# RWKV-6 attention and a gated feed-forward layer: idle products out of the first stage, two blocks of small products moved on TensorE

## The chip, the cores and the metric

The kernel runs on one core of one Trainium2 chip. The metric is the time of one execution on the device in microseconds (us), lower is better; a kernel's time is the median of its runs. The core has five engines with an instruction list each: PE (TensorE, matrix products; PEld is its loading of the stationary operand), DVE (VectorE), ACT (ScalarE), POOL (GpSimd) and SP (SyncE, which here only issues DMAs).

## The reference

Two blocks in a row, all in float32. First a recurrence over 768 tokens for 4 batches and 8 heads of width 48, then a feed-forward layer with an unusual activation over the 3072 tokens of width 384:

```python
for t in range(S):
    cur = np.einsum('bhd,bhe->bhde', u[None] * kt, vt)
    y[:, :, t] = np.einsum('bhd,bhde->bhe', rt, state + cur)
    state = wt[:, :, :, None] * state + np.einsum('bhd,bhe->bhde', kt, vt)
...
h = x @ w_in                                              # x: y as (3072, 384); w_in: (384, 2048)
sp = np.maximum(h, 0.0) + np.log1p(np.exp(-np.abs(h)))    # softplus
g = h * erf(sp)
return (g @ w_out).astype(np.float32)                     # w_out: (2048, 384)
```

## The kernel before

**Steps.** The 768 tokens are cut into 12 steps of 64 tokens; a step holds all 32 heads. `attend_first` (line 853) does step 0, `attend` (line 984) steps 1 to 4, `attend_late` (line 803) steps 5 to 11.

**Inside a step.** The decayed products of r and k of two tokens of a step are not made token by token but in six levels: level n takes the pairs of tokens that lie in the two halves of one block of 2^n tokens. Per level, `level_products` (line 646) issues 32 small matmuls into one of two PSUM banks (`products`, line 132, hands them out in turn), `take_level` (line 664) or a masked multiply puts what belongs to the level into the tile `own`, and `scale` (line 319) multiplies r and k by the decay of the level, in place, so that the next level can use them. Level 1 uses copies of r and k into which u is multiplied (`prepare`), so it needs nothing of `scale`. The decays themselves are made on POOL (line 357).

**From a step's products to x.** `from_own` (line 681) multiplies `own` by v into the PSUM tile `y`, in two halves called swap 1 and swap 0, 16 matmuls each. `fence` (line 697) is a small DVE copy that reads `y` between the halves. `through_state` (line 704) adds r times the state of the steps before (32 matmuls, line 713; nothing in step 0), copies `y` out on ACT (lines 721, and 741 or 751) and makes x transposed, `xT`. In steps 1 and later the rows that lie on other partitions are moved by six DMAs (line 757). In step 0 that is done by `hop` (line 726): three matmuls with a constant (`shift`, line 732) and three DVE additions (line 746). `state_part` (line 762) makes k times v of the step (32 matmuls, line 769), and `next_state` (line 620) adds it to the faded state on DVE, which step s+1 reads.

**Feed-forward.** `hidden` (line 1097) multiplies `w_in` by `xT` (line 1130, moving operand 256 columns wide) and ACT copies the result (line 1139); softplus and erf run on ACT; `project` (line 1161) and, from step 3 on, `project_fast` (line 1243) multiply by `w_out`. Pieces of these stand between the levels of a later step, so that PE has wide products to do while DVE scales.

**Weights.** `w_in` and `w_out` arrive as 64-bit words and are turned into float32 by ACT, DVE and POOL (`convert`, line 221, lines 259, 261, 267, 276, 281, 289) during steps 0 to 3. Each load of a pair of weight tiles is held back by a one-element copy (lines 240, 242) until some other result is there; `stages["l"](2, seen[:, 0:1])` in line 925, for example, stands behind the fence of step 0.

**What sets the order.** Everything lies in a manual schedule: on every engine the instructions stand in the order of the Python calls, and semaphores hold an instruction back until its inputs are there. Nothing overtakes on an engine. A float32 matmul of the program is recorded as two passes, each with a load of weights and a matmul, so PE executes four instructions for one call. The instructions themselves are brought to the core by DMA, on queues of their own.

**Products without a use.** Before the first real product PE runs 36 matmuls of 64x64 on the identity (line 1522, `FEW`) and five of 128x256 (`stay_warm`, line 967); two more `stay_warm` follow each half of level 1. Behind levels 2 to 5 of step 0 stands one product of 384 columns with a zero operand (`keep_busy`, line 976), which writes into the bank that the next level overwrites.

**The places that the change touches.** At the end of `attend_first`, after the products of level 6 (line 911), three eighths of the level 1 products of step 1 stand ahead of `from_own(0, own, 1)` (line 916) and five eighths between `through_state` and `hop` (line 940). At the end of `attend`, for steps 1 to 4, the order on PE is swap 1, the transposes of k (line 1051), a piece of `hidden`, `state_part`, swap 0, a piece, `through_state`.

Of the kernel before, what the change touches and what calls it, by code (L numbers as in the profile page):

```python
# [11 lines left out]
FP32 = mybir.dt.float32  # L12
# [5 lines left out]
P = 128  # L18
FAST = 3
EP = 64  # L20
HC = 64
NC = 2
NJ = 2
FG = 8
FT = 2
FEW = 36

# [33 lines left out]
def kernel(  # L63
# [14 lines left out]
    nc = tc.nc  # L78
    PSUM = bass.MemoryType.PSUM

    n_steps, _, _, JP, C = rkw.shape
# [4 lines left out]
    _, NT, DM = w_out.shape  # L86
# [27 lines left out]
    ident = const.tile([P, P], FP32, name="ident")  # L114
# [17 lines left out]
    def products(shape, n=None):  # L132

        if n is None:
            n = turns["next"]
            turns["next"] = 1 - n
        names = "abc"[: len(shape) - 1]
        return banks[n][:].rearrange(
            f"p ({' '.join(names)}) -> p {' '.join(names)}", **dict(zip(names, shape[1:]))
        )  # L140
# [167 lines left out]
    def rows(e, n=D):  # L308
        return slice(e * EP, e * EP + n)
# [336 lines left out]
    def level_products(pp, rk, level, ns=range(NJ * NP)):  # L646

        half = 1 << (level - 1)
        m = HC - half if 1 < level <= MASKED else HC if level == 1 else half
        for n in ns:  # L650
            for s0 in range(0, C, HC):
                for e in range(NE):
                    right = rk(0, n)[rows(e), s0 : s0 + HC]
                    to = pp[s0 : s0 + m, e, n, :]
                    if level > 1:
                        right = rights(right, half)
                        to = to[:, : HC // 2].rearrange("p (b h) -> p b h", h=half)
                    nc.tensor.matmul(  # L658
                        to, lhsT=rk(1, n)[rows(e), s0 : s0 + m], rhs=right,
                        start=True,  # L660
                        stop=True,
                    )
# [18 lines left out]
    def from_own(s, own, swap):  # L681
        vt = loaded[s][1]
        for j in range(NJ):
            for q in range(0, NP, 2):
                for h in range(NC):
                    e = h ^ swap
                    for p in (q, q + 1):
                        n = j * NP + p
                        t = slice(h * HC, (h + 1) * HC)
                        nc.tensor.matmul(  # L690
                            y[at(e, p), e, p // 2, j, t],
                            lhsT=vt[t, n * NE + e, :], rhs=own[t, e * JP + n, :],
                            start=swap == 1 and not j and not q, stop=True,
                            skip_group_check=True,
                        )
# [157 lines left out]
    def attend_first(xT):  # L853


        for _ in prepare(0):
            pass
        totals = plan_totals(0)
        _, vt, made, _, _ = parts_of(0)
        t5 = turns["first"]  # L860
        own = att.tile([P, NH, HC], FP32, name="own")
        halves = [range(j * NP, (j + 1) * NP) for j in range(NJ)]
        batch = JP * C // 2 // NJ
        pp = products([P, NE, JP, HC])
        for half in halves:
            level_products(pp, by_pair(made), 1, half)
            stay_warm(2)
        nc.scalar.copy(first[:], mask_sb[:, 0, :])
        totals(1, part=slice(0, batch))
        for j in range(NJ):  # L870
            scale(0, 1, batch=j)
        load_second(t5[:, 1, 0, NP - 1, 1:2])

        def wait_for(t):

            nc.gpsimd.tensor_copy(out=block_sb[:, 0:1], in_=t5[:, 1, 0, NP - 1, t : t + 1])

        wait_for(1)
        totals(1, part=slice(batch, 2 * batch))
        totals(2, part=slice(0, batch // 2))  # L880
        nc.vector.tensor_mul(
            own[:], pp[:].rearrange("p e n t -> p (e n) t"),
            first[:, None, :].to_broadcast([P, NH, HC]),
        )
        behind = {3: (3,), 4: (4, 5), 5: (6,)}
        for level in range(2, LOG):
            pp = turns.pop("pp", None) or products([P, NE, JP, HC])
            for j, half in enumerate(halves):
                level_products(pp, first_pair, level, half)
                scale(0, level, batch=j)  # L890
            turns["pp"] = products([P, NE, JP, HC])
            keep_busy(turns["pp"])
            take_level(own, pp, level)
            wait_for(1 << level - 1)
            if level == 2:
                totals(2, part=slice(batch // 2, batch))
            else:
                totals(*behind[level])
            if level == 2:
                stages["b"](0, 0)  # L900
                stages["b"](0, 1)
                stages["r"](0)
                for _ in prepare(1):
                    pass
                nc.sync.dma_start(out=vt[:], in_=v[0])
                stages["l"](1, own[:, 0, 2:3])
                nc.sync.dma_start(out=ws[1][:], in_=rkw[1][:, 2])
        totals = plan_totals(1)
        pp = turns.pop("pp")
        for half in halves:  # L910
            level_products(pp, first_pair, LOG, half)
        half = 1 << LOG - 1
        got, of = pp, own[:].rearrange("p (e n) t -> p e n t", e=NE)
        turns["pp"] = products([P, NE, JP, HC])
        second = by_pair(ready[1][0])
        level_products(turns["pp"], second, 1, range(3))
        for swap in (1, 0):
            for h in range(NC):
                some, e = slice(h * HC, h * HC + half), h ^ swap
                nc.scalar.copy(of[some, e, :, half:], got[some, e, :, :half])  # L920
        stages["h"](0)
        stages["h"](0)
        from_own(0, own, 1)
        fence()
        stages["l"](2, seen[:, 0:1])
        load_v(1)
        stages["o"](0)
        stages["b"](1, 0)
        stages["b"](1, 1)
        from_own(0, own, 0)  # L930
        view_k = view(t5[:, 0, 1], 0, [[2 * NP * C, NJ], [HC, NP * NC], [1, HC // 2]])
        tot = ready[0][1][LOG - 1]
        nc.vector.tensor_mul(
            view_k, view_k, view(tot, 1, [[NP * C >> LOG - 1, NJ], [2, NP * NC], [0, HC // 2]])
        )
        stages["h"](1)
        stages["h"](1)
        totals(1)
        through_state(0, xT)
        level_products(turns["pp"], second, 1, range(3, JP))  # L940
        turns.pop("hop")()
        stages["r"](1)
        stages["o"](1)
        totals(*range(2, LOG + 1))
        kT = att.tile([P, NH, D], FP32, name="kT", bufs=1)

        def turn():

            ps = products([P, JP, P], turns["next"])
            for n in range(JP):  # L950
                nc.tensor.transpose(ps[:, n, :], first_pair(1, n), ident[:])
            nc.scalar.copy(
                kT[:].rearrange("p (e n) d -> p e n d", e=NE),
                ps[:].rearrange("p n (e d) -> p e n d", e=NE)[..., :D],
            )
            send("br")
            load_third()
            stages["l"](5, kT[:, 0, 0:1])

        def to_state():  # L960
            ps = products([P, NC, JP, HC], turns["next"])
            state_part(0, kT, ps)
            next_state(0, ps)

        turns["pending"] = {2: turn, 3: to_state}
# [7 lines left out]
                start=True, stop=True,  # L973
            )

    def keep_busy(pp):

        zeros = states[0][:].rearrange("p h n d -> p (h n d)")
        nc.tensor.matmul(
            pp[:].rearrange("p e n t -> p (e n t)")[:, :DM], lhsT=ident[:],  # L980
            rhs=zeros[:, :DM], start=True, stop=True, skip_group_check=True,
        )

    def attend(s, xT, early, place, behind):
# [61 lines left out]
                nc.sync.dma_start(out=loaded[2][0][:, level - 3], in_=rkw[2][:, level - 3])  # L1046

        from_own(s, own, 1)
        ps = products([P, JP, P])
        for n in range(JP):  # L1050
            nc.tensor.transpose(ps[:, n, :], K[:, n, :], ident[:])  # L1051
# [10 lines left out]
            for _ in range(3):  # L1062
                mixing.send(nc.vector)

        ps = products([P, NC, JP, HC])
        state_part(s, kT, ps)
        from_own(s, own, 0)
        next_state(s, ps)
        for _ in following:
            pass  # L1070
        place(LOG + 1)
        through_state(s, xT)
        behind()

    later, chunks, started = [], [], []
# [435 lines left out]
    for kk in range(KT):  # L1511
        n = D // KT
# [3 lines left out]
    with tc.manual_schedule(  # L1516
        engines={getattr(mybir.EngineType, x) for x in ("PE", "DVE", "Activation", "Pool", "SP")}
    ):
        few = ps_m.tile([P, NC, P], FP32, name="m")
        for n in range(FEW):  # L1520
            here = rows(n & 1, HC)
            nc.tensor.matmul(
                few[here, 0, :HC], lhsT=ident[here, here], rhs=ident[here, here],
                start=True, stop=True,
            )
        stay_warm(5)
        for t in states:
            nc.gpsimd.memset(t[:], 0.0)
        nc.gpsimd.memset(over_blocks[:], 1.0)
# [176 lines left out]
```

## Time and profile before

| | |
|---|---|
| time, median of 3 runs | 585.51 us (583.67 to 587.04) |
| the profiled execution: its own time | 584.51 us |
| its span, first to last instruction | 582.7 us |
| mean granted TensorE clock | 0.994 |
| busy: PE, PEld, DVE, ACT, POOL | 98%, 85%, 73%, 61%, 42% |
| instructions recorded | 16637, of which 7304 matmul passes and as many loads of weights |

A row of the timeline is: start in us, length in us, engine, line, operation, output<-inputs, shape of weights, shape of moving operand, number of passes; in brackets the idle time of the engine before it and what the profile takes for its release. "issue" as a releaser means that the engine waited for nothing that the profile shows. Ends of matmuls are modelled, so a row may seem to reach into the next. In a table of stretches the columns are start and end, length, busy time of PE, PEld, DVE, ACT and POOL with the number of instructions, the granted clock of TensorE, the share of the 16 DMA engines that were busy, and GB/s.

How PE's time lies by stage, from such a table (busy of PE in each stretch):

| stretch, us | what | PE busy | clock |
|---|---|---|---|
| 2.00 to 8.40 | idle products | 6.40 of 6.40 | 1.00 |
| 8.40 to 21.40 | step 0, levels 1 to 6 | 11.49 of 13.00 | 1.00 |
| 21.40 to 30.40 | end of step 0, first products of step 1 | 6.58 of 9.00 | 0.62 |
| 30.40 to 65.50 | step 1, first half of step 2 | 34.33 of 35.10 | 1.00 |
| 65.50 to 100.00 | steps 2 and 3 | 34.25 of 34.50 | 1.00 |
| 100.00 to 582.70 | the rest | 479.22 of 482.70 | 1.00 |

### The profile page before, as it was taken

The page shows a single profiled execution, that of the slowest core. Times are in us where ns is not written, and L with a number is a line of the kernel's source. Part 1 is how long each engine was busy: PE and PEld are TensorE (multiplying, and loading weights), DVE is VectorE, ACT ScalarE, POOL GpSimd, SP SyncE. Part 2 cuts the span into 40 slices and gives each one's busy share as a digit, 9 for nine tenths or more (in the row PEclk, how much of TensorE's full clock was granted, in tenths as well). Part 3 has the DMA queues.
Part 4 walks back from the last instruction along what each step waited for, and adds up shares of the span by engine and source line. Part 5 has one row for each costly group of instructions (what it writes and reads, how often), then busy time and mean ns, then how long its engine had stood idle before and what let it go on. Part 6 is the DMA issues. An engine that isn't in the chain of part 4 may idle for free.

```text
span 582.7 us, 16637 instructions
## 1 busy us (share of the span) xinstructions
PE 572.3 (98%) x7304; PEld 493.7 (85%) x7304; DVE 426.8 (73%) x451; ACT 355.0 (61%) x478; POOL 242.1 (42%) x263
## 2 busy tenths in 40 slices
PE   8799999999999999999999999999999999999997
PEld 7588787678668758898898898898898899988997
DVE  7585794899795699699599599599599526356640
ACT  3567778635544597766766666665765761388700
POOL 3378273612793786276176077077074000000000
PEclk9799999999999999999999999999999999999999
DMA  7497472540435215236236336235331101000111
GB/s 258 137 340 268 158 235 67 207 154 12 145 79 163 86 48 181 46 119 191 47 112 197 47 110 199 46 110 163 47 108 29 19 10 36 0 2 1 28 28 27
DMA packets 52057, 62.04 MB, mean 106 GB/s; under 512 B 33392, under 2 KB 38800, under 8 KB 50960
## 3 DMA queue, kind: packets, MB, share of 16 engines
q1 hardware_dynamic: 51360, 60.58, 33.9%
q8 instruction: 57, 0.93, 0.6%
q10 hardware_dynamic: 624, 0.39, 0.3%
q14 instruction: 16, 0.13, 0.1%
HBM read 51.60 MB, written 8.27 MB: 103 GB/s over the span
## 4 chain that ended last, share of the span: by engine, by line
PE 86%; DMA 2%; DVE 0%; ACT 0%; issue 0%; SPq 0%; ACTq 0%
PE m L1130 31%; PE m L1243 28%; PE m L1161 11%; PE pp L1331 4%; PE pp L658 3%; PE y L1331 2%; PE y L690 2%; PE y L713 2%; PE pp L769 1%; DMA words<-in_moe_w_out 1%; PE pp L1051 1%; PE pp L1243 0%; DMA xT<-y 0%; PE pp L782 0%; DVE y L276 0%; DVE w_out_sb L281 0%
## 5 line engine op out<-in xcount | busy, mean ns | idle before, releaser
L1130 PE MATMUL m<-xT,w_in_sb 128*128 128x256 f32 x960 | 214.2, 381 | 1.0 <-ACT y L261 0.8
L1130 PEld LDWEIGHTS m<-xT,w_in_sb 128*128 128x128 f32 x960 | 180.0, 190 | 26.2 <-ACT y L261 0.8
L335 DVE TENSOR_TENSOR in<-in,tot_sb 128x1024 f32<-128x1024 f32 (+1 forms) x55 | 77.0, 1399 | 21.3 <-PE pp L658 20.7
L1139 ACT COPY h<-m 128x512 f32<-128x512 f32 x80 | 46.2, 580 | 63.0 <-PE m L1130 62.8
L1161 PE MATMUL m<-w_out_sb,h 128*128 128x384 f32 x192 | 64.3, 491 | 0.0
L1161 PEld LDWEIGHTS m<-w_out_sb,h 128*128 128x128 f32 x192 | 35.7, 190 | 23.5
L1243 PE MATMUL m<-mixed,h 128*128 128x192 f32 x256 | 45.6, 331 | 0.0
L1243 PE MATMUL m<-w_out_sb,h 128*128 128x192 f32 x256 | 44.8, 329 | 0.0
L1243 PEld LDWEIGHTS m<-mixed,h 128*128 128x128 f32 x256 | 41.4, 190 | 0.9
L1090 ACT ACT_TABLE_LOAD x30 | 38.5, 1283 | 5.9 <-DVE h L1095 5.4
L1243 PEld LDWEIGHTS m<-w_out_sb,h 128*128 128x128 f32 x256 | 41.6, 190 | 0.3
L658 PEld LDWEIGHTS pp<-in 48*48 48x48 f32 (+4 forms) x2368 | 30.3, 120 | 13.5 <-issue 6.8
L1243 PE MATMUL m<-w_out_sb,room 128*128 128x192 f32 x240 | 41.5, 326 | 0.0
L465 POOL TENSOR_TENSOR words<-words,own 128x384 f32<-128x384 f32 x21 | 31.0, 1476 | 22.5 <-DVE words L496 12.8
L1086 ACT ACT_TABLE_LOAD x30 | 38.5, 1283 | 2.3 <-issue 1.8
L458 POOL TENSOR_TENSOR own<-rest 128x384 f32<-128x384 f32 x7 | 10.4, 1481 | 71.0 <-ACT o L1249 59.7
L506 POOL TENSOR_TENSOR words<-words 128x384 f32<-128x384 f32 x28 | 39.7, 1446 | 0.0
L1243 PEld LDWEIGHTS m<-w_out_sb,room 128*128 128x128 f32 x240 | 39.4, 190 | 0.0
L658 PE MATMUL pp<-in 48*48 48x32 f32 (+4 forms) x2368 | 34.1, 206 | 2.1 <-issue 2.1
L618 POOL COPY faded<-s 128x1 f32<-128x1 f32 x10 | 12.4, 1240 | 54.5 <-DVE s L624 54.5
L531 DVE TENSOR_REDUCE sums<-rk 128x16 f32<-128x768 f32 (+2 forms) x31 | 31.7, 1022 | 0.0
L506 POOL TENSOR_TENSOR rk<-words 128x384 f32<-128x384 f32 x28 | 31.5, 1153 | 0.0
(202 smaller groups left out, 990.4 us busy)
## 6 DMA issues: line engine op xcount, KB each, us to landing
in<-in_rkw SPq DMA_DIRECT2D x8, 1024.0 KB, 5.0
words<-in_moe_w_in SPq DMA_DIRECT2D x16, 384.0 KB, 5.3
words<-in_moe_w_out SPq DMA_DIRECT2D x16, 384.0 KB, 6.2
words<-in_rk_rows SPq DMA_DIRECT2D x8, 768.0 KB, 7.2
w<-in_rkw SPq DMA_DIRECT2D x11, 512.0 KB, 6.5
v<-in_v SPq DMA_DIRECT2D x12, 384.0 KB, 5.4
out<-o SPq DMA_DIRECT2D x45, 96.0 KB, 2.5
in<-in_rkw SPq DMA_DIRECT2D x7, 512.0 KB, 5.8
```

The lines of the kernel that those rows point to most:

```text
L335: nc.vector.tensor_mul(halves, halves, view(tots[level - 1], 0, [[1, n], [2, nb], [0, half]]))
L465: engine.tensor_mul(to, to, of[:, :, None, :].to_broadcast([P, NEAR // 2 // half, half, D]))
L506: engine.tensor_mul(to[:, i], r[:, half:], k[:, part * rows + i, None].to_broadcast([P, half, D]),)
L531: nc.vector.tensor_reduce(out=to, in_=of, axis=mybir.AxisListType.X, op=ALU.add)
L658: nc.tensor.matmul(to, lhsT=rk(1, n)[rows(e), s0 : s0 + m], rhs=right, start=True, stop=True,)
L1086: nc.scalar.activation(sp_room, chunks[0], AF.Softplus)
L1090: nc.scalar.activation(at, sp_room, AF.Erf)
L1130: nc.tensor.matmul(ps[:, ff, :], lhsT=w_in_sb[:, g * FG + f + ff, kk * P : (kk + 1) * P], rhs=xT[:, kk, :], start=kk == 0, stop=kk == KT - 1,)
L1139: nc.scalar.copy(h[:, f : f + FT, :], ps[:])
L1161: nc.tensor.matmul(ps[j][:], lhsT=gs[g][:, f, j * C : (j + 1) * C], rhs=w_out_sb[:, g * FG + f, :], start=g + f == 0, stop=g == NG - 1 and ...
L1243: nc.tensor.matmul(to, lhsT=a[:, f], rhs=b[:, f], start=start and f == 0, stop=f == FG - 1, skip_group_check=True,)
L1331: nc.tensor.matmul(to[:, e], lhsT=a[:, 2 * i + e], rhs=b, start=start and not k, stop=True, skip_group_check=True,)
```

## The change

- The 36 matmuls of 64x64 at the start go; `stay_warm` runs six times in place of five.
- Behind level 6 of step 0, the three eighths of the level 1 products of step 1 are replaced by one `keep_busy` of 256 columns (it now takes its width). All 32 matmuls of that level stand in one piece behind the three `shift` products of `hop`, so swap 1, swap 0 and the shifts of step 0 follow each other on PE.
- In step 1 alone, `state_part` and `next_state` stand behind `through_state`: on PE swap 1, transposes, a piece of `hidden`, swap 0, a piece, `through_state`, `state_part`; on DVE `next_state` directly ahead of the first `scale` of step 2, as before with nothing between them. A `fence` is added between swap 1 and swap 0 of step 1.

No other engine's list changes its order: DVE gains the one fence; ACT, POOL and SP have the same instructions in the same order. PE loses 72 passes at the start and gains two there and two behind level 6.

```diff
-FEW = 36
@@ attend_first
         turns["pp"] = products([P, NE, JP, HC])
         second = by_pair(ready[1][0])
-        level_products(turns["pp"], second, 1, range(3))
+        keep_busy(turns["pp"], NC * P)
         for swap in (1, 0):
...
         through_state(0, xT)
-        level_products(turns["pp"], second, 1, range(3, JP))
         turns.pop("hop")()
+        level_products(turns["pp"], second, 1)
         stages["r"](1)
@@ keep_busy
-    def keep_busy(pp):
+    def keep_busy(pp, n=DM):
         zeros = states[0][:].rearrange("p h n d -> p (h n d)")
         nc.tensor.matmul(
-            pp[:].rearrange("p e n t -> p (e n t)")[:, :DM], lhsT=ident[:],
-            rhs=zeros[:, :DM], start=True, stop=True, skip_group_check=True,
+            pp[:].rearrange("p e n t -> p (e n t)")[:, :n], lhsT=ident[:],
+            rhs=zeros[:, :n], start=True, stop=True, skip_group_check=True,
         )
@@ attend
         from_own(s, own, 1)
+        if s == 1:
+            fence()
         ps = products([P, JP, P])
...
-        ps = products([P, NC, JP, HC])
-        state_part(s, kT, ps)
+        def to_next():
+            ps = products([P, NC, JP, HC])
+            state_part(s, kT, ps)
+            return ps
+
+        ps = to_next() if s > 1 else None
         from_own(s, own, 0)
-        next_state(s, ps)
+        if s > 1:
+            next_state(s, ps)
         for _ in following:
             pass
         place(LOG + 1)
         through_state(s, xT)
+        if s == 1:
+            next_state(s, to_next())
         behind()
@@ the start
-        few = ps_m.tile([P, NC, P], FP32, name="m")
-        for n in range(FEW):
-            here = rows(n & 1, HC)
-            nc.tensor.matmul(
-                few[here, 0, :HC], lhsT=ident[here, here], rhs=ident[here, here],
-                start=True, stop=True,
-            )
-        stay_warm(5)
+        stay_warm(6)
```

## The prediction

> **What bounds the kernel now.** I read the page first: engines, granted clock, DMA queues.
>
> ```profile
> span 582.7 us, 16637 instructions
> PE 572.3 (98%) x7304; PEld 493.7 (85%) x7304; DVE 426.8 (73%) x451; ACT 355.0 (61%) x478; POOL 242.1 (42%) x263
> PEclk9799999999999999999999999999999999999999
> q8 instruction: 57, 0.93, 0.6%
> ```
>
> PE is busy 98% of the span, and the chain that ended last is PE work from 76 us on; what it waits for before that is small (0.77 us at 65.49, 0.25 us at 75.94). So a microsecond gained before the first product of the feed-forward layer (30.40 us) reaches the end, unless it is given back on the way. The page also shows one slow slice of the clock, and a queue q8 that brings instructions: 57 packets for 14608 recorded instructions of PE, so 256 instructions or 128 passes to a packet. The second view is PE's timeline up to 30 us:
>
> ```profile
> 2.00 4.10 PE L1522 MATMUL m<-ident 64*64 64x64 f32 x72 [2.00 <-POOL ident masks.py:199]
> 6.03 2.43 PE L971 MATMUL m<-ident 128*128 128x256 f32 x10
> 8.38 0.69 PE L658 MATMUL pp<-rk 48*64 48x64 f32 x32
> ...
> 18.10 0.91 PE L979 MATMUL pp<-s,ident 128*128 128x384 f32 x2 [1.11 <-DVE in L328]
> 18.94 0.92 PE L658 MATMUL pp<-in 48*48 48x32 f32 x64
> 19.79 0.91 PE L979 MATMUL pp<-s,ident 128*128 128x384 f32 x2
> 20.64 0.79 PE L658 MATMUL pp<-in 48*32 48x32 f32 x60
> 23.47 0.32 PE L658 MATMUL pp<-in 48*32 48x32 f32 x4 [2.05 <-issue]
> 23.72 0.92 PE L658 MATMUL pp<-rk 48*64 48x64 f32 x24
> 24.42 1.32 PE L690 MATMUL y<-own,v 64*48 64x64 f32 x32
> 26.10 1.11 PE L690 MATMUL y<-own,v 64*48 64x64 f32 x32 [0.37 <-DVE seen L699]
> 26.95 1.32 PE L658 MATMUL pp<-rk 48*64 48x64 f32 x40
> 28.20 1.93 PE L732 MATMUL m<-y,mixed 128*128 128x256 f32 x4
> 29.97 0.59 PE L732 MATMUL pp<-y,mixed 128*128 128x256 f32 x2
> ```
>
> Level 6 stops after 60 of its 64 passes, for 2.05 us, with no releaser. Between the pass that starts at 18.10 and the one at 23.47 lie 2+64+2+60 = 128 passes: one packet. Looked up window by window, q8's packets start at 10.51, 15.66, 21.12 and 24.61 us, each about 0.95 long; PE goes on 2.44 us after the second and 2.35 us after the third. So both stalls (1.11 and 2.05 us) are PE waiting for its own instructions, the one put down to DVE too. The packet starts after PE crosses the previous limit: 13.64 to 15.66, 18.10 to 21.12, and 23.47 to 24.61 when the data queues are idle. From one limit to the instructions behind the next it takes 4.46, 5.37 and 3.5 us (1.14+2.35).
>
> ```profile
> 16.21:19.62 3.41, 2.30 (x124) 1.65 (x116) 2.51 (x4) 2.15 (x6) 1.20 (x5) 1.00 0.87 252
> 19.62:23.03 3.41, 1.80 (x85) 1.10 (x74) 2.83 (x5) 0.00 (x0) 0.35 (x2) 1.00 0.38 138
> 23.03:26.44 3.41, 2.60 (x73) 2.35 (x77) 0.66 (x2) 2.46 (x6) 0.42 (x1) 0.50 0.02 5
> 26.44:29.86 3.42, 3.42 (x75) 3.03 (x68) 1.40 (x4) 2.22 (x7) 3.21 (x4) 0.50 0.64 201
> ```
>
> The third view is stretches of 3.41 us laid on the clock's steps (the first figure after the length is PE busy, the third from the end the clock). After a stretch with 1.80 us of PE work the clock is halved, for 6.83 us; 2.30 us keeps it up; 3.42 us brings it back. All of the end of step 0 runs in that half-speed time.
>
> **Part 1: the start.** 72 passes (4.10 us) go, two of 128x256 come. A wide pass takes 0.24 us in the ten at 6.03 and 0.48 at half clock (1.93/4 at 28.20); 12 passes from 2.00 on end between 4.9 and 7.8. I take 6.9, half of them at each price, since the 64x64 passes at 57 ns are slower than the 64-column passes of level 1 (0.69/32 = 22 ns). The first L658 needs a DVE copy that ends at 6.49, so it starts at 6.5 to 7.8 in place of 8.38: -1.5 taken. It passes through levels 1 to 3, where DVE waits for PE (1.47 us before its first masked product).
>
> **Part 2: the limits of the packets move.** With 70 passes fewer, each limit falls 70 passes later in the work: the one in level 3 (13.64) falls 6 passes into level 4, the one at 18.10 falls 2 passes into level 6, and the one inside level 6 falls at the very end of swap 0 (4 passes of level 6, 2 of `keep_busy`, 64 of `from_own`). Level 4 without a stall would start at 15.97-1.5 = 14.5; its instructions are due 3.5 to 5.4 after a limit that is crossed at about 10.5, so 14.0 to 15.9; 15.1 taken. Level 6: due 18.6 (15.1+3.5) to 21.3 (15.9+5.4), wanted at about 19; 20.3 taken (15.1+5.2), with queues busy as at 18.10. It then runs through, 0.8 us, to 21.1. ACT's four copies (L920, 1.52) and two conversions (L259, 1.07) end at 23.7. Swap 1 (0.66 at full clock), the fence (0.17) and swap 0 stand behind the copies and end at 23.4; the last pass of swap 0 is due 20.3+3.5 = 23.8. ACT's copy of `y` (0.37) follows, so `hop` starts at 24.2 in place of 28.20. The bounds, level 6 at 19.2 and a quick packet or at 21.3 and a slow one, and 0.5 for the copy: 19.2+3.5+0.5 = 23.2 and 21.3+5.4+0.5 = 27.2.
>
> **Part 3: the end of step 0.** PE has `hop` (6 passes) and 64 passes of level 1 before the first L1130. At full clock 6x0.24 + 64x0.0163 (1.04/64, rows of L658) = 2.5: 26.7 in place of 30.40, **-3.7**. At half clock 1.93+0.59 and 64x0.033 (1.32/40), 4.6 together: 28.8, and part of the 12 passes behind (2.75 us at full clock) is slow too: -0.9. The removed 24 passes, the 40 that move and the `keep_busy` (0.47, under ACT's copies, 1.52) are in these sums. DVE's three additions end 0.5 behind `hop`, under the 64 passes. POOL's copy behind the fence and its add (L289, 1.81), for which L1130 waits, go with the fence, from 26.02 to about 23, and end at 25. ACT, POOL and SP keep their order, so the weight loads that hang on the fence and on `hop` start as much earlier; their share of the DMA engines in 23.5 to 27 is 0.02, so they have room.
>
> [...]
>
> [...]
>
> **Part 4: later limits.** From step 1 on, each limit lies 68 passes later. Five stretches between limits then are short by the old timeline: 33.7 to 38.8, 38.8 to 43.7 and 74.8 to 79.8 (5.1, 4.9, 5.0 us, busy queues) and, with the new order, 57.9 to 61.2 and 61.2 to 64.5 (3.2 and 3.3, idle queues). Against 3.5 to 5.4 they cost 0 to 0.5 each: +0.4 to +1.8; **+0.9** taken. The old timeline has two such stretches without a stall (41.6 to 46.6, 58.4 to 61.8), so zero is possible too.
>
> **Part 5: step 1.** `through_state` ends 0.94 us earlier on PE (L769, 64 passes at 57.34). But ACT is held by softplus until 60.6 and L1139 until 61.1, and copied `y` at 61.32: 0.2 earlier. The wait for `xT` at 65.49 (0.77) shrinks by that: **-0.2**, bounds -0.77 and +0.3. `next_state` (0.95) now waits for L769 until about 61.3, and the scaling of step 2 (L335, 1.22) is queued behind it on DVE: done at 63.5, just before the level 2 products at 63.61 want it; +0.3 if it is late. The fence (0.17) lies in 6.2 us in which DVE is idle, with 2.8 us of L1130 between it and swap 0: nothing.
>
> **Sum.** -3.7+0.9-0.2 = -3.0 us. The profiled execution took 584.51 (1.8 of it outside the span), so 581.5 by its own time; the median of the runs lies 1.0 above it, and from that the forecast is 582.5 us. The runs before spread over 3.4 us, as a stray clock or packet would make them.
>
> **Rivals.** *The clock falls all the same.* Before level 6 PE would wait about 1.3 us for its packet, then 0.3, 0.25 and 0.8 around swaps 1 and 0: some 3.41 us stretches hold 1.8 to 2.2 us of work, between the row that fell (1.80) and the row that held (2.30). For it: nothing fills the wait of level 6. Against: no single gap is as long as 2.05, and `keep_busy` fills one. Then -0.9+0.9-0.2 = -0.2: 585.3.
>
> *Slower: the packets come late.* In place: levels 4 and 6, whose packets now fall into the loads of 14 to 20 us (queues 0.88 busy at 18.10 to 21.10). If each takes 5.4 us or more, `hop` starts at 27.2 with the clock down, L1130 at 31.8 (+1.4), and part 4 costs its 1.8: 588.7. It decides from `hop` later than about 26.
>
> *Better: packets quick and clock up.* `hop` at 23.7, L1130 at 26.2 (-4.2), nothing in part 4, -0.77 in part 5: 580.5.
>
> *No effect*, a start hidden by DMA: against it, L328 at 7.73 already has its data, and the 2.05 us lie behind the loads.
>
> **How the numbers follow.** Forecast 0.45, clock falls 0.33, better 0.12, slower 0.10. About 0.5% (2.93 us) is what a measurement of this kernel tells from no change, so faster means under 582.6, slower over 588.4. The forecast sits on that line: 0.27 of its 0.45 count as faster, with nearly all of better: 0.38. Clock-falls and the rest of the forecast are the same: 0.50. Slower, with a tail of clock-falls: 0.12. The range 580.3 to 587.0 takes in the three larger cases and leaves out most of slower and the far end of better.
>
> **What would show it.** Right: `hop` (L732) near 24 and the first L1130 near 27 with the clock at 1.00; level 6 in one piece, with the stall at its head; L658 of level 1 at about 7. Wrong: a clock of 0.50 over `hop`; stalls without a releaser near 39, 44, 61 or 79; level 4 or 6 later than 16 and 21.5; or a first L1130 that is early and a product at 65 that is not.

## The result and the profile after

| | before | after |
|---|---|---|
| median of 17 runs each, us | 585.29 (583.08 to 587.11) | 582.62 (579.64 to 585.09) |
| ratio, with its 95% interval | | 0.9951 (0.9933 to 0.9968) |
| profiled execution: own time, span, us | 584.51, 582.7 | 582.62, 580.7 |
| mean granted clock of the profiled execution | 0.994 | 0.997 |

The changed kernel is 0.5% faster; the forecast was 582.5 us. The page of the changed kernel has the same shape as before, with one slow slice of the clock:

```profile
span 580.7 us, 16502 instructions
PE 571.8 (98%) x7236; PEld 491.5 (85%) x7236; DVE 427.8 (74%) x452; ACT 354.9 (61%) x478; POOL 242.5 (42%) x263
PEclk9899999999999999999999999999999999999999
```

PE's timeline of the changed kernel, which answers to the one shown of before:

```profile
2.00 5.49 PE L970 MATMUL m<-ident 128*128 128x256 f32 x12 [2.00 <-POOL ident masks.py:199]
7.42 0.75 PE L657 MATMUL pp<-rk 48*64 48x64 f32 x32
...
15.07 1.03 PE L657 MATMUL pp<-in 48*56 48x32 f32 x64
...
18.72 0.92 PE L657 MATMUL pp<-in 48*32 48x32 f32 x64
19.81 0.70 PE L978 MATMUL pp<-s,ident 128*128 128x256 f32 x2 [0.17 <-DVE own L667]
20.44 0.86 PE L689 MATMUL y<-own,v 64*48 64x64 f32 x32
21.66 0.66 PE L689 MATMUL y<-own,v 64*48 64x64 f32 x31 [0.37 <-DVE seen L698]
23.50 0.25 PE L689 MATMUL y<-own,v 64*48 64x64 f32 x1 [1.18 <-issue]
24.21 1.68 PE L731 MATMUL m<-y,mixed 128*128 128x256 f32 x4 [0.46 <-ACT y L720]
25.68 1.06 PE L731 MATMUL pp<-y,mixed 128*128 128x256 f32 x2
26.67 1.78 PE L657 MATMUL pp<-rk 48*64 48x64 f32 x64
28.38 2.86 PE L1138 MATMUL m<-xT,w_in_sb 128*128 128x256 f32 x12
```

Level 6 (18.72) now runs in one piece. Both stalls of before (1.11 us ahead of level 5 and 2.05 us inside level 6) are gone, and a new one of 1.18 us without a releaser stands before the last pass of swap 0. `hop` starts at 24.21 in place of 28.20, the first product of the feed-forward layer at 28.38 in place of 30.40. Between the two lies a stretch at half clock, which the table of stretches shows:

```profile
21.24:24.66 3.42, 1.41 (x36) 1.08 (x35) 1.79 (x4) 2.03 (x7) 3.08 (x3) 1.00 0.46 129
24.66:28.07 3.41, 3.41 (x58) 2.49 (x60) 2.06 (x4) 2.95 (x6) 2.23 (x3) 0.50 1.02 361
```

PE works for 1.41 us in the first of them, and the clock is halved for the second; in before the half-speed time was two stretches long (23.03 to 29.86). From 28.38 on the order of events is that of before, 2.0 us earlier, up to the wait in front of step 2's products: 0.50 us at 63.38, where before had 0.77 at 65.49 (the first row is of before):

```profile
65.49 5.45 PE L1130 MATMUL m<-xT,w_in_sb 128*128 128x256 f32 x24 [0.77 <-ACT y L261]
...
63.38 5.44 PE L1138 MATMUL m<-xT,w_in_sb 128*128 128x256 f32 x24 [0.50 <-ACT y L260]
```

From there to the end it stays 2.0 to 2.1 us. So the profile pair has the whole difference of span (2.0 us) in the first 28.4 us. That is one pair of executions; the runs below show that it is not how every execution goes.

### The profile page after: what moved, and what is told of

The parts are those of the page before. It is cut to its first block, busy times and chain, and to the rows that moved or that the text cites. A ratio compares the mean times of both kernels' runs of the same rounds, so it can differ in the third digit from the quotient of the medians.

```text
span 580.7 us, 16502 instructions
## 1 busy us (share of the span) xinstructions
PE 571.8 (98%) x7236; PEld 491.5 (85%) x7236; DVE 427.8 (74%) x452; ACT 354.9 (61%) x478; POOL 242.5 (42%) x263
## 4 chain that ended last, share of the span: by engine, by line
PE 84%; DVE 3%; DMA 2%; issue 1%; ACT 0%; SPq 0%; ACTq 0%
PE m L1138 30%; PE m L1251 28%; PE m L1169 9%; PE pp L1339 4%; PE pp L657 3%; PE y L1339 2%; PE y L689 2%; PE y L712 2%; PE pp L768 1%; DMA words<-in_moe_w_out 1%; PE pp L1052 1%; DVE in L334 0%; PE pp L1251 0%; DVE words L464 0%; DVE y L275 0%
## 5 line engine op out<-in xcount | busy, mean ns | idle before, releaser
L1138 PE MATMUL m<-xT,w_in_sb 128*128 128x256 f32 x960 | 214.3, 382 | 0.7 <-ACT y L260 0.5
L1138 PEld LDWEIGHTS m<-xT,w_in_sb 128*128 128x128 f32 x960 | 180.2, 190 | 25.6 <-ACT y L260 0.6
L657 PEld LDWEIGHTS pp<-in 48*48 48x48 f32 (+4 forms) x2368 | 30.1, 120 | 11.6 <-issue 4.3
L657 PE MATMUL pp<-in 48*48 48x32 f32 (+4 forms) x2368 | 33.9, 206 | 0.1
```

The source lines that it names most:

```text
L657: nc.tensor.matmul(to, lhsT=rk(1, n)[rows(e), s0 : s0 + m], rhs=right, start=True, stop=True,)
L1138: nc.tensor.matmul(ps[:, ff, :], lhsT=w_in_sb[:, g * FG + f + ff, kk * P : (kk + 1) * P], rhs=xT[:, kk, :], start=kk == 0, stop=kk == KT - 1,)
```

## The experiments

All ratios are to the kernel before, run on the same chip. The kernel before took 586.65 us there in the first four runs, 585.35 in the next four, 585.56 in the next two and 586.11 in the last two (medians of 29, 19, 11 and 16 runs). The theories to tell apart: **limits** (the gain comes from where the limits between PE's instruction packets fall, with the clock behind them), **order** (it comes from the order of swaps, `hop` and level 1), **start** (it comes from the shorter start alone).

### One part at a time

`only_few` is the kernel before with the first edit alone:

```diff
-        few = ps_m.tile([P, NC, P], FP32, name="m")
-        for n in range(FEW):
...
-        stay_warm(5)
+        stay_warm(6)
```

> The kernel before with the start alone changed: no 64x64 products, six stay_warm. Theory (limits): what counts is where the 128-pass limits of PE's instruction packets fall. With 70 passes fewer ahead of it the limit inside level 6 falls 10 passes into swap 0 of step 0, so levels 5 and 6 run without the stalls of 1.1 and 2.05 us, a stall of 1 to 2 us shows inside swap 0, and the first product of the feed-forward layer starts near 28.5: ratio to the kernel before about 0.995 to 0.997 (582.3 to 583.5 us). Rival (order): the order of level 1, swaps and shifts is what gained; then this one has only the shorter start, 0.9 us at most, 0.9985 (584.4 us).

Measured: 581.76 us, ratio 0.9918 (0.9892 to 0.9945), more than was expected. `only_level1` has the second edit alone (level 1 of step 1 in one piece behind `hop`, `keep_busy` of 256 columns in its old place).

> The kernel before with level 1 of step 1 behind the three shifts and a product of 256 columns in the place of the first three eighths; the 36 small products stay. Limits: the limit stays inside level 6, so the stall of about 2 us and the half clock stay and the time is within 0.5 us of the kernel before (ratio 0.999 to 1.001, 585 us). Order: most of the gain is here, 0.9965 or less (583.2 us).

Measured: 588.35 us, 1.0025 (1.0005 to 1.0045), slower than either theory had it. `only_state` has the third alone (step 1's state products and the addition to the state behind `through_state`, with the fence).

> The kernel before with the state products of step 1 behind through_state, and the fence. By the prediction's part 5: the wait at 65.49 shrinks by 0.2 us, ratio 0.9997, not to be told from 1 (585.1 us). Rival (state): x of step 1 leaves 0.9 us earlier and all of it counts, 0.9985 (584.4 us).

Measured: 584.26 us, 0.9959 (0.9938 to 0.9980), better than either theory had it. PE's timelines of `only_few` (first fence) and `only_level1` (second):

```profile
18.68 0.92 PE L657 MATMUL pp<-in 48*32 48x32 f32 x64
...
21.62 0.33 PE L689 MATMUL y<-own,v 64*48 64x64 f32 x8 [0.37 <-DVE seen L698]
24.68 0.89 PE L689 MATMUL y<-own,v 64*48 64x64 f32 x24 [2.73 <-issue]
...
28.60 2.75 PE L1129 MATMUL m<-xT,w_in_sb 128*128 128x256 f32 x12
```

```profile
20.07 0.91 PE L658 MATMUL pp<-in 48*32 48x32 f32 x60
23.64 0.25 PE L658 MATMUL pp<-in 48*32 48x32 f32 x4 [2.65 <-issue]
...
49.56 0.29 PE L658 MATMUL pp<-in 48*48 48x32 f32 x8 [2.53 <-issue]
```

With the small products gone, the limit falls some 70 passes later: the last 4 of level 6, the 24 of level 1, the 32 of swap 1 and the first 8 of swap 0 run ahead of it (68 by this count), and there the stall stands, 2.73 us long. With the level 1 move alone the stall stays before the last four passes of level 6, a second one of 2.53 us stands at 49.56 us, and the kernel is no faster. So the first edit alone is enough for the gain, and the order theory falls.

### The limits put back

`limits_back` is the changed kernel with 36 products of one column at the start and two calls of `stay_warm` less. Nothing else differs, and the start is no longer than in the changed kernel (first L657 at 6.50).

```diff
-        stay_warm(6)
+        few = ps_m.tile([P, NC, P], FP32, name="m")
+        for n in range(36):
+            here = rows(n & 1, HC)
+            nc.tensor.matmul(
+                few[n & 1 and HC : (n & 1 and HC) + 1, 0, :1],
+                lhsT=ident[here, :1], rhs=ident[here, :1], start=True, stop=True,
+            )
+        stay_warm(4)
```

> The changed kernel, with the limits put back to where they lie in the kernel before: 36 products of one column and four stay_warm at the start, which are the same number of PE instructions as the 36 small products and five stay_warm less one, while the first real product starts near 7 to 8 us as in the changed kernel. Limits: the stalls of about 1.1 and 2 us in levels 5 and 6 come back and most of the gain is lost, ratio 0.998 to 1.000 (584 to 585.3 us). Order: the order of the changed kernel is untouched, so the ratio stays at 0.995 (582.6 us).

Measured: 585.61 us, 0.9991 (0.9972 to 1.0010). Its timeline has the stall of before back, two passes further on:

```profile
18.49 0.79 PE L657 MATMUL pp<-in 48*32 48x32 f32 x62
21.89 0.25 PE L657 MATMUL pp<-in 48*32 48x32 f32 x2 [2.62 <-issue]
...
30.38 0.92 PE L1138 MATMUL m<-xT,w_in_sb 128*128 128x256 f32 x3
```

The clock was at 0.50 from 23.15 to 29.97. With the order of the changed kernel and a start that is 1.9 us earlier than before, the first product of the feed-forward layer comes at 30.38, where before had 30.40. So the limits theory stands, and the start theory falls: PE arrives earlier at the limit (level 6 starts at 18.49, in before at 20.64) and waits longer there (2.62 us, in before 2.05).

Counting PE's passes from the first one of the program shows the same in every profile that has a stall of this kind. This one stands behind 478 passes in before, `only_level1`, `only_state` and `limits_back`, behind 477 in the changed kernel and behind 476 in `only_few` and `few_state`; the stalls without a releaser at 34 and 47 to 50 us, which the runs below show too, stand behind 731 and behind 985 or 986. The place goes with the count of the passes, and not with the work that happens to stand there.

### The limit pushed past `hop`, and the same kernels again

`wide_warm` makes the warming products half as many and twice as wide, so that the limit of the 1.18 us stall falls behind `hop`.

```diff
-        stay_warm(6)
+        stay_warm(3)
@@ each half of step 1's level 1
-            stay_warm(2)
+            stay_warm(1)
@@ stay_warm: 512 columns in place of 256
-        ps = ps_m.tile([P, NC, P], FP32, name="m")
+        ps = ps_m.tile([P, 2 * NC, P], FP32, name="m")
```

> The changed kernel with its warming products made of half as many, twice as wide: three of 512 columns at the start for six of 256, and one of 512 behind each half of the second step's level one for two of 256. The work in the array is the same, but each limit between instruction packets falls 10 passes later in the order of the work, so that the one that held the last pass of swap 0 falls 4 passes into step 1's level one, behind hop. Limits theory: the 1.18 us stall (issue) at swap 0's last pass is gone, hop starts at 22.9 to 23.3 in place of 24.21, a stall turns up behind it or none (the instructions are due near 23.5), and the clock has one stretch fewer at half or the same one: 1.0 to 2.5 us faster than the changed kernel, ratio to the kernel before 0.991 to 0.993. Theory that the order of the products made the gain: as the changed kernel, 0.995.

Measured: 581.82 us, 0.9946 (0.9923 to 0.9969). The stall before `hop` is gone as expected, `hop` starts even earlier than expected, and the clock stays up; but the time is that of the changed kernel, and not the 0.991 to 0.993 that was expected. What took it shows further on in PE's timeline:

```profile
20.80 0.67 PE L689 MATMUL y<-own,v 64*48 64x64 f32 x32 [0.37 <-DVE seen L698]
22.06 1.13 PE L731 MATMUL m<-y,mixed 128*128 128x256 f32 x4 [0.59 <-ACT y L720]
...
24.64 2.86 PE L1138 MATMUL m<-xT,w_in_sb 128*128 128x256 f32 x12
...
34.10 0.57 PE L768 MATMUL pp<-v,kT 64*48 64x48 f32 x31 [0.54 <-issue]
...
48.25 0.25 PE L657 MATMUL pp<-in 48*32 48x32 f32 x4 [2.61 <-issue]
```

3.7 us ahead of the changed kernel's first profile at 24.64, then 0.54 and 2.61 us of stalls at two later limits: the head start is given back. The changed kernel itself, run again, gives back its head start in the same way.

> The changed kernel once more, for comparison on this chip. Ratio to the kernel before 0.993 to 0.997; the stall before swap 0's last pass between 0.8 and 1.5 us, and the clock at half somewhere between 23 and 29 us unless the clock's stretches fall otherwise.

Measured: 582.20 us, 0.9956 (0.9940 to 0.9971).

```profile
20.73 0.80 PE L689 MATMUL y<-own,v 64*48 64x64 f32 x32 [0.37 <-DVE seen L698]
22.00 1.13 PE L731 MATMUL m<-y,mixed 128*128 128x256 f32 x4 [0.46 <-ACT y L720]
...
24.58 2.86 PE L1138 MATMUL m<-xT,w_in_sb 128*128 128x256 f32 x12
...
34.31 0.67 PE L768 MATMUL pp<-v,kT 64*48 64x48 f32 x41 [0.94 <-issue]
...
47.23 0.32 PE L657 MATMUL pp<-in 48*32 48x32 f32 x14 [1.26 <-issue]
```

The same program, 3.80 us further at its first feed-forward product than in its first profile. The packet for the last pass of swap 0 started at 18.98 us (21.18 in the first profile), so that the stall there was under 0.2 us and not the 0.8 to 1.5 us that was expected, and the clock stayed up. Of these 3.80 us, 2.86 were gone at 48 us, 2.2 of them at the limits at 34 and 47 us, and in the end its span is 0.7 us shorter. The kernel before also shows a second face:

> The kernel before, profiled on this chip. Limits theory: the same stalls as in its first profile (1.1 us before level 6, 2.0 to 2.7 us before the last four passes of level 6), because the places are set by the program. What differs between two profiles, late stalls without a releaser at 40 to 65 us above all, is what the executions of one kernel differ by; if one stands at 57 to 63 us, it would explain why moving the state products gave 2.4 us where the profile has 0.5.

Measured: 585.32 us (one run).

```profile
22.74 0.25 PE L658 MATMUL pp<-in 48*32 48x32 f32 x4 [1.27 <-issue]
...
47.16 0.29 PE L658 MATMUL pp<-in 48*48 48x32 f32 x6 [1.49 <-issue]
...
66.31 3.91 PE L1130 MATMUL m<-xT,w_in_sb 128*128 128x256 f32 x17 [1.08 <-ACT y L261]
```

The stall in level 6 stands at the same place, 0.8 us shorter, with 1.25 us of lead from 27 to 42 us; then a stall at 47 us that the first profile did not have, and a longer wait for ACT. The places are the program's; the lengths differ from execution to execution.

`few_state` is the changed kernel without the move of level 1 (both halves where before had them).

> The changed kernel without the move of level one (its two halves stand where they stood before, with the shorter idle product): the removed start and the moved state products alone. If the parts add up as measured alone (0.9918 and 0.9959), 0.988. If the state products give only what their profile showed (0.5 us), 0.991. If the level one move is needed to keep the limits off the critical work, 0.995 or more. The profile should show the stall 8 passes into swap 1, as with the start removed alone, and no wait at the products near 64 us.

Measured: 582.58 us, 0.9951 (0.9933 to 0.9969), the ratio of the changed kernel. The parts do not add up, and the move of level 1 adds nothing that these runs show: without it the stall stands 8 passes into swap 0 as in `only_few`, 1.35 us long, and a second one of 1.52 us at 49.07.

### What the later stalls wait for

In the changed kernel's second profile, the limit ahead of the one at 34 us was crossed at 27.99, and the packet started at 31.94; for the one at 47 us these are 41.17 and 44.87. In between, the data queues ran at 363 and 411 GB/s. `w2_later` moves one load of 512 KB from ahead of the first packet to behind it. `loads_later` does so too, issues another load of 512 KB some 7 us later, and moves 896 KB from ahead of the second packet to behind it:

```diff
@@ hop
-                load_w(2)
@@ attend, behind a level
-            if s == 1 and level in (3, 4):
-                nc.sync.dma_start(out=loaded[2][0][:, level - 3], in_=rkw[2][:, level - 3])
+            if s == 1 and level == 3:
+                load_w(2)
+            if s == 1 and level in (3, 6):
+                nc.sync.dma_start(out=loaded[2][0][:, level // 6], in_=rkw[2][:, level // 6])
@@ place
-                    if (s, n) == (1, LOG - 1):
+                    if (s, n) == (1, LOG + 1):
                         load_w(3)
                         load_v(2)
```

> The changed kernel with one load moved: the 512 KB of step 2's decays go out about 7 us later (behind step 1's level 3 in place of behind hop). Theory that the head start is given back at later packet limits because PE's instruction packets stand behind the data that the queues hold: the packet for the limit in step 0's state products (34 us) is asked for at 28.0 and came at 31.9, when the loads issued by then had gone through; 512 KB at 400 GB/s are 1.3 us, so that it comes near 30.6 and the stall of 0.5 to 0.9 us there is gone in a run whose clock does not fall. The bytes ahead of the next packet that hurts (45 us) are the same, so the stall at 47 to 48 us stays at 1.2 to 2.6 or grows by what the first one gave: the time is that of the changed kernel, ratio 0.994 to 0.996. Theory that the stalls have nothing to do with data: both stalls as before.

> The changed kernel with three loads moved, 512 KB of decays as in the run beside it, one of the two halves of step 2's keys and receptances from behind step 1's level 4 to behind its level 6 (39 to about 48 us), and step 3's decays and step 2's values from 45 to about 55 us. Now 512 KB less stand before the packet near 45 us too. Give-back theory: both stalls (34 and 47 us) shrink by 1.3 us each at most, to under 0.4 and under 1.3; 1 to 2 us faster than the changed kernel, ratio 0.991 to 0.994, unless the wait for ACT's softplus at 62 to 63 us takes it: then that wait shows 0.5 to 1.5 us there and the ratio stays 0.995. Theory that the stalls have nothing to do with data: as the changed kernel, 0.995, with both stalls.

Measured: `w2_later` 581.09 us, 0.9926 (0.9898 to 0.9953); `loads_later` 581.41 us, 0.9928 (0.9908 to 0.9949). `loads_later` was run again:

> The changed kernel with the three loads moved, once more. If the stalls at 34 and 47 us are what it gains by: none or under 0.5 us at either place, 28 to 61 us passed in 32 to 33 us (34.9 with the stalls), ratio 0.991 to 0.994; if its first time was chance, 0.995 as the changed kernel.

Measured: 580.81 us, 0.9924 (0.9900 to 0.9947). PE's timeline of `loads_later` over the two places:

```profile
32.85 1.08 PE L657 MATMUL pp<-in 48*60 48x32 f32 x64
33.75 0.91 PE L767 MATMUL pp<-v,kT 64*48 64x48 f32 x64
...
44.77 1.00 PE L657 MATMUL pp<-in 48*32 48x32 f32 x64
45.70 2.86 PE L1139 MATMUL m<-xT,w_in_sb 128*128 128x256 f32 x12
```

Both groups run in one piece. The two packets started 2.09 and 2.46 us after the limit before theirs was crossed, in place of 3.95 and 3.70. The clock stayed up, and the span is 578.3 us (578.7 in the second run), against 580.0 of the changed kernel's second profile, whose clock stayed up too.

That the stall at 47 us is PE waiting for instructions that stand behind data is shown by a pair with nearly the same head start. `no_state`, a run further down, has its loads where the changed kernel has them, and the order on PE differs only behind 50 us. It has its first feed-forward product at 26.22 us, and `loads_again` at 25.98. The second packet started at 45.67 us in the one and at 42.43 in the other (rows of level 6 of step 1, `no_state` first):

```profile
48.27 0.32 PE L657 MATMUL pp<-in 48*32 48x32 f32 x14 [2.04 <-issue]
...
45.34 0.76 PE L657 MATMUL pp<-in 48*32 48x32 f32 x64
```

For the limit at 34 us it is not shown: `no_state` has no stall there either, its packet started some 2.2 us after the limit with the loads unmoved, and `loads_later` was 0.83 us less far ahead than the changed kernel's second profile. `w2_later` kept a stall of 0.67 us at 49.25 us and none at 34, as expected, but its time is as good as that of `loads_later`, which was not. Its profile had a half-speed stretch, so it doesn't show the case that was meant, and six runs are few: how the gain divides between the moved loads stays open. The version with the moved loads is 0.75% faster than before. By its ratio it is faster than the changed kernel too (0.9951 and 0.9956), but the intervals overlap, and the two were not run on the same chip.

### Without the third edit

`no_state` is the changed kernel with the state products and the addition where before had them, without the fence.

> The changed kernel without its second part: step 1's state products and the addition to the state stand where they stood before (in front of the second swap, without the fence). The prediction's price for that part (0.2 us): ratio to the kernel before 0.994 to 0.997, as the changed kernel, and a wait in front of the products near 63 to 65 us of 0.5 to 0.9 us. The price that the part had in the times when it was made alone (2.4 us, 0.9959): ratio 0.998 to 1.0. Theory that PE's early gain runs into ACT's softplus and the transfer of x there, and that the moved products are what lets it through: a wait of 1.0 to 2.5 us in front of step 2's first products (60 to 66 us), ratio 0.997 to 0.999.

Measured: 582.92 us, 0.9955 (0.9930 to 0.9980): no loss that the runs show. Its profile waited 0.30 us near 65 us, and 2.04 us for instructions at 48.27, and behind that its clock fell at a new place:

```profile
45.26:48.67 3.41, 1.37 (x67) 0.90 (x66) 1.03 (x2) 1.80 (x4) 2.92 (x6) 1.00 1.03 400
48.67:52.08 3.41, 3.41 (x9) 2.70 (x10) 1.23 (x1) 1.13 (x2) 2.07 (x3) 0.50 0.35 138
```

### Where the gain lies

Each run lists its mean granted clock, and one stretch of 3.41 us at half speed lowers it by 0.003 (0.997 in the first profile of the changed kernel, which has one, 0.994 in that of before, which has two); so the runs can be sorted by the number of such stretches:

| half-speed stretches | before: runs, mean us | after: runs, mean us | moved loads: runs, mean us |
|---|---|---|---|
| 0 | 4, 583.48 | 11, 581.51 | 8, 580.66 |
| 1 | 5, 584.81 | 9, 582.58 | 4, 582.17 |
| 2 | 48, 585.90 | 3, 584.10 | |
| 3 or 4 | 18, 587.44 | 1, 585.09 | |
| all | 75, 586.07 | 24, 582.38 | 12, 581.17 |

Inside a kernel one stretch costs 1.23 us (slope over all 190 runs of the study that list it). Before has 2.15 of them on the mean, after 0.75: 1.40 x 1.23 = 1.7 of the 3.7 us between the means. But the 3.7 us mix chips, and before is 1.3 us slower on the chip of the first four runs than in the next four. On the chip of `after_again` alone the means are 585.39 us with 1.95 stretches (19 runs) and 582.34 us with 0.43 (7 runs): 1.52 x 1.23 = 1.9 of 3.05 us come with the clock. The other 1.2 us stand at equal clock, and no run here divides them between shorter stalls and the rest.

`only_few` has the times of the changed kernel at equal numbers (581.49 and 582.66 with 0 and 1 stretches); its better ratio is against a slower kernel before, on another chip. Whether it is faster than the changed kernel is not shown, since the two were not run on the same chip. Nor is it shown that the second and third edit gain anything once the first is made: without the one the ratio is 0.9951 (`few_state`), without the other 0.9955 (`no_state`), with neither 0.9918 (`only_few`).

## Why the prediction was right, and where not

The time (582.5 against 582.62) came out by the mechanism that was named: stalls for instruction packets, whose places the removed passes move, and the clock behind them (in the first profiles 2.05 us inside level 6 before, 1.18 us ahead of the last pass of swap 0 after, and two half-speed stretches against one). Several of its terms were wrong and cancelled, so that an agreement within 0.2 us is luck: the first profile has the clock of the rival without the later stalls, the second the clock of the forecast with more of them.

- **Part 1, the start.** -1.5 was taken; the first L657 came at 7.42 (-0.96) in the first profile and at 6.55 in the second. The same twelve wide passes ahead of it took 5.49 and 4.59 us; the clock rose at 7.59 and at 5.54 us. Both starts lie inside the bounds, 6.5 to 7.8. By itself the earlier start is worth nothing (`limits_back`, 0.9991).
- **Part 2, the places.** Right: no stall inside level 6, the new one exactly before the last pass of swap 0, that pass at 23.50 (23.8), `hop` at 24.21 (24.2). Level 4 came at 15.07 (15.1), but by luck: the forecast had it at 14.5 and 0.6 us of waiting for its packet, and in the profile it did not wait and PE's start had gained 0.5 us less. Failed: "20.3 taken (15.1+5.2)" for level 6. There was no stall at its head. The limit before was crossed at 15.13 and the packet started at 15.66; with 2.3 us from there, an estimate from the 2.44 and 2.35 us of before, its instructions came after 2.8 us, and the rows show that they were there at 18.74 when PE wanted them. That 3.5 is not the least, `before_again` shows: there PE passed from one limit (14.56) over the next (17.85) without a wait, 3.3 us in all. The early level 6 was made up for by the next packet, which took 4.76 us (18.74 to 23.50) and not 3.5. The same step was sized too tightly at the other end as well: 5.4 was taken as the most, and 6.0 (`only_few`, 18.70 to 24.68) and 6.9 us (`wide_warm`, 41.37 to 48.25) occurred. The part that is steady is from the start of a packet to PE going on, 2.2 to 2.6 us in the stalls shown above; the time from the limit to the start of the packet varies, from 0.4 us (`before_again`, 14.56 to 14.97) to 4.6 (`wide_warm`, 41.37 to 45.94).
- **Part 3, the clock.** The forecast had the clock up, its rival down. Both occur: 11 of 24 runs of the changed kernel have no half-speed stretch, 9 have one. In the first profile the rival's case came (first L1138 at 28.38, 28.8 predicted), in the second the forecast's (24.58, 26.7 predicted). The rival's 585.3 was too slow: one stretch costs 1.2 us, and the runs with one have a mean of 582.58. It was priced with all of `hop` and level 1 at half speed and more of the products behind it; in the profile the clock rose at 28.07.
- **Part 4, later limits.** +0.9 was taken of 0 to 1.8. It is 0 in the first profile and 2.2 in the second. The kind was right (packets late behind busy queues, shown at 47 us by `no_state` and `loads_again`), and one place: the first of the five stretches ends at the limit at 34 us. The limit at 47 us was not among them, and the other four showed 0.4 us at most. What the step lacked is that it depends on part 3: the more PE is ahead, the more it waits at the limits, so that the execution with the clock up was 3.8 us ahead of the other at 24.6 us and 0.9 at 48.
- **Part 5, the state products.** -0.2 was taken and stands in the changed kernel (`no_state` 0.9955). In the kernel before, the same edit alone gave 0.41% (0.20 to 0.62), more than the 0.77 us that the wait allowed. The second profile of before has 1.08 there, `only_state` none, and the latter's runs have 1.75 half-speed stretches on the mean against 2.38 of before on that chip, 0.8 us: 1.6 to 1.9 us together, inside the interval of 1.2 to 3.6. What makes this edit idle once the start is changed was not seen.
- **The rivals.** "The clock falls all the same" is half of the truth. "Slower: the packets come late" had its place wrong (the packets for level 6 started 0.5 and 0.7 us after the limit in the two profiles), and its threshold was never reached: `hop` came between 22.0 and 24.5 in all six profiles with the changed kernel's limits.

## What to carry to other kernels

Where PE runs many small passes, count its instructions: here a packet came for about every 256 of them (57 for the 14608 recorded in before), PE stalled at a limit for up to 2.73 us, and with 70 idle passes fewer the stall of level 6 stood 8 passes into swap 0 (both `only_few`). Keep bulk loads out of the microseconds in which a packet is fetched, as `loads_again` did at 47 us: its packet started at 42.43 us, with the loads unmoved at 45.67 (`no_state`). To put the limits into stretches of long passes follows from the same, but was not tried here by itself. A gain ahead of such limits can be given back at later ones: of the 3.80 us that lay between the two profiles of the changed kernel at 24.6 us, 2.86 were gone at 48. So look for it again some 20 us further on, and in more than one profiled execution.

## What was not expected

**Where the clock fell.** In stretches of 3.41 us laid on the clock's steps (in the first profiles of before and after it fell 17.07 us, five stretches, after it first rose, and stayed at half for 6.83 and 3.41 us), PE was busy 0.52, 0.77, 1.14, 1.26, 1.37, 1.41, 1.67, 1.80, 1.81 and 1.82 us in ten that were followed by half speed during the steps (`only_few`, `only_level1`, `only_state`, `limits_back`, `no_state`, after, `w2_later`, and the two profiles of before with `few_state`), and 1.76, 1.87, 1.92, 2.04, 2.05 and more in those that were not (`only_level1`, `wide_warm`, `before_again`, `loads_again`, `no_state`). These are the two with the least work that kept the clock there:

```profile
47.91:51.32 3.41, 1.76 (x15) 1.56 (x15) 1.34 (x2) 2.43 (x4) 0.85 (x3) 1.00 1.01 402
```

```profile
46.71:50.12 3.41, 1.87 (x12) 1.65 (x13) 1.22 (x1) 1.15 (x2) 0.94 (x5) 1.00 0.36 138
```

(the first of `only_level1`, the second of `wide_warm`.) The longest gap does not tell the two apart: a gap of 2.61 us that was split between two stretches (`wide_warm`) left the clock up, and one of 1.27 us (`before_again`) did not. The work within a stretch does better, but it draws no sharp line: 1.76 us kept the clock where 1.80 to 1.82 did not, and at the end of `loads_later` even 1.48 us did, since the stretch behind it still has the full clock:

```profile
573.32:576.73 3.41, 1.48 (x10) 1.18 (x8) 0.35 (x1) 0.00 (x0) 0.00 (x0) 1.00 0.41 106
576.73:580.14 3.41, 0.00 (x0) 0.00 (x0) 0.00 (x0) 0.00 (x0) 0.00 (x0) 1.00 0.04 10
```

Those that kept it with 1.48 to 1.87 us hold 7 to 10 passes of 192 or 256 columns, and those that lost it with 1.41 to 1.82 us at most four wide passes among many small ones. So the kind of pass may count beside its time; no run tests that. The stretches start where the clock first rose, between 5.5 and 8.2 us after the span's start in the profiles, 5.97 in before and 7.59 in after; with that, the same gaps fall into one stretch or are split between two.

**How much one program differs from itself.** Two executions of the changed kernel stood 3.80 us apart at 24.6 us and 0.7 us apart at the end. In these profiles the limits late in the loading phase work as a leveller: the execution that is ahead waits there.
